# A chunked RWKV and two-MoE kernel on one core: bonus term of six units through TensorE, inverse decay on ScalarE, another start for units 0 and 1

## Chip, core and metric

One core of a Trainium2 chip (trn2) runs the whole program. The metric is the device time of one launch in microseconds. Engine names are those of the profile: PE is TensorE (PEld its weight loads), ACT is ScalarE, DVE is VectorE, POOL is GpSimd, SP is SyncE; the `q` of SPq or ACTq marks an engine's issue of DMAs.

## What is computed

A linear-attention recurrence with decay and a bonus term, then two MLPs on its output (batch 4, 8 heads, 768 steps, head size 48):

```python
for t in range(S):
    cur = einsum('bhd,bhe->bhde', u * kt, vt)            # bonus
    y[t] = einsum('bhd,bhde->bhe', rt, state + cur)
    state = wt[..., None] * state + einsum('bhd,bhe->bhde', kt, vt)
x = y.transpose(0, 2, 1, 3).reshape(3072, 384)
x = relu(x @ w_in) ** 2 @ w_out                          # d_ff 2048
out = ((x @ w_a) * (x @ w_b)) @ w_out2                   # d_ff 1536
```

All inputs are float32, uniform decays between 0.8 and 0.95.

## The kernel before

The sequence is cut into 6 chunks of 128 steps. A unit is one chunk of one batch, 24 in all, with 8 heads as 4 groups of 2. `prepare(i)` does the part of a unit that needs no TensorE. A forward scan on DVE (L197) gives the running product f of the decays; a reciprocal of its last column (L201) and a scan backwards (L202) give its inverse q. Then r is multiplied by f (L206), k by q (L208), and one Newton step corrects q (L209, L210); ACT squares f and q into a range check (L218). POOL multiplies r, k and u (L220, L221), DVE sums over the head (L223), and ACT writes that sum `dd` as a diagonal into the matrix A, one activation a head (L226): this is the bonus term. `scores(i)` makes the score matrices on PE (L239), transposes k (L243), and DVE copies the scores over A's diagonal under a mask (L247). `mix(i)` multiplies A with v (L267), adds the state's part from the second chunk on (L261), and makes the new state (L274, L292, L294). The result x is copied from PSUM (L284), and six small DMAs move the last 16 of each head pair into place (L287).

Units are gathered in tiles: tile 0 holds units 0 and 1 (256 tokens), five tiles hold four units, the last one two. The first MLP runs tile by tile in 16 steps: `hp` (L417 in tile 0, L311 to L313 after), its square on ACT and DVE (L423, L424; later L463, L464, L371, L372), and `acc` (L410; L311 to L313). While tile n runs, the units of tile n+1 are prepared. Tile 0 works in float32, the later ones split each operand into two fp32r parts and make three products. Weights arrive as 64-bit words and are decoded in four instructions, ACT, DVE, ACT, DVE (L41 to L44), two tiles of weights a step of tile 0. The second MLP starts when the first is through.

The program is written in this order, and a scheduler with its own cost estimates interleaves it on every engine; units 0 and 1 have higher priority (offset 100). On the chip each engine runs its instructions strictly in the order so found, so what waits holds everything behind it. Pools set the number of buffers: `A` 2, `fq` 1, PSUM 3 `acc`, 2 `mm` and 3 `at` banks.

Of the kernel before, what the change touches and what calls it, by code (L numbers as in the profile page):

```python
# [8 lines left out]
F32 = mybir.dt.float32  # L9
# [3 lines left out]
AF = mybir.ActivationFunctionType  # L13
ALU = mybir.AluOpType
AX = mybir.AxisListType

B, H, S, D = 4, 8, 768, 48
# [3 lines left out]
C = 128  # L21
# [3 lines left out]
G = 4  # L25
GP = 112
T = B * C
HP = 100
BURSTS = (0, 2, 4, 6, 7, 9, 11, 13)
LOW = 2.0 ** -52  # L30
LIM = 2.0 ** 102
# [40 lines left out]
def chunked_path(ctx, tc, flags, krT, wT, krn, vn, u, w1, w2, w3, w4, w5, out):  # L72
    nc = tc.nc
    pe, act, dve, pool, sync = nc.tensor, nc.scalar, nc.vector, nc.gpsimd, nc.sync
    PS = bass.MemoryType.PSUM

    const = ctx.enter_context(tc.tile_pool(name="const", bufs=1))
# [5 lines left out]
    at = ctx.enter_context(tc.tile_pool(name="at", bufs=1))  # L83
    dr = ctx.enter_context(tc.tile_pool(name="dr", bufs=1, space=bass.MemoryType.DRAM))
    p_acc = ctx.enter_context(tc.tile_pool(name="p_acc", bufs=3, space=PS))
    p_mm = ctx.enter_context(tc.tile_pool(name="p_mm", bufs=2, space=PS))
# [7 lines left out]
    mask = const.tile([128, 1, 128], F32, name="mask")  # L94
    d1 = const.tile([GP, G, C + 1], F32, name="d1")
    ones = const.tile([GP, 1], F32, name="ones")
    d2 = const.tile([GP, G, C + 1], F32, name="d2")
    half = const.tile([GP, 1, 2], F32, name="half")
    u_bc = const.tile([128, DM], F32, name="u_bc")
    chk = const.tile([GP, NU], F32, name="chk")  # L100
# [69 lines left out]

    loaded = {}

    def load_unit(i):
        b, c = units[i]
        w = ld.tile([GP, G * (C + 1) + 1], F32, tag="lw", name="lw")
        kr = ld.tile([GP, 2, G, C], F32, tag="lkr", name="lkr")
        v = ld.tile([128, H, D], F32, tag="vn", name="vn", bufs=3)
        nn = ld.tile([128, 2, H, D], F32, tag="nn", name="nn")
        r0 = b * S + c * C
        sync.dma_start(out=w, in_=wT[b, c])  # L180
        sync.dma_start(out=kr, in_=krT[b, c])
        sync.dma_start(out=v, in_=vn[r0:r0 + C].rearrange("p (h d) -> p h d", h=H))
        sync.dma_start(out=nn, in_=krn[r0:r0 + C].rearrange("p n (h d) -> p n h d", h=H))
        loaded[i] = w, kr, v, nn

    xt = {}
    tiles = [(0, 1)] + [tuple(range(i, i + 4)) for i in range(2, NU - 2, 4)] + [(NU - 2, NU - 1)]
    x0 = {}
    unit = {}

    def prepare(i):
        b, c = units[i]
        w, kr, v, nn = loaded.pop(i)
        k, r = kr[:, 0], kr[:, 1]
        fq = at.tile([GP, 2, G * (C + 1)], F32, tag="f", name="fq")
        f, q = (fq[:, n].rearrange("p (g t) -> p g t", g=G) for n in range(2))
        dve.tensor_tensor_scan(  # L197
            out=fq[:, 0], data0=w[:, :-1], data1=d1.rearrange("p g t -> p (g t)"),
            initial=0.0, op0=ALU.mult, op1=ALU.max,
        )  # L200
        dve.reciprocal(out=d2[:, :, C:], in_=f[:, :, C:])  # L201
        dve.tensor_tensor_scan(  # L202
            out=fq[:, 1, ::-1], data0=w[:, 1:][:, ::-1], data1=d2.rearrange("p g t -> p (g t)")[:, ::-1],
            initial=0.0, op0=ALU.mult, op1=ALU.add,
        )
        dve.tensor_tensor(out=r, in0=r, in1=f[:, :, 0:C], op=ALU.mult)  # L206
        e = w[:, 0:G * C].rearrange("p (g t) -> p g t", g=G)
        dve.tensor_tensor(out=k, in0=k, in1=q[:, :, 1:], op=ALU.mult)  # L208
        dve.tensor_tensor(out=e, in0=f[:, :, 1:], in1=q[:, :, 1:], op=ALU.mult)  # L209
        dve.scalar_tensor_tensor(  # L210
            out=k, in0=e, scalar=2.0, in1=k, op0=ALU.subtract, op1=ALU.mult, reverse0=True
        )
        pe2 = at.tile([GP, G, 2, 1], F32, tag="pe2", name="pe2", bufs=2)
        dve.tensor_tensor(
            out=pe2[:, :, :, 0], in0=f[:, :, C:C + 1].to_broadcast([GP, G, 2]),
            in1=half.to_broadcast([GP, G, 2]), op=ALU.mult,
        )
        act.activation(out=fq, in_=fq, func=AF.Square, accum_out=chk[:, i:i + 1])  # L218
        p = nn[:, 0]
        pool.tensor_tensor(out=p, in0=p, in1=u_h, op=ALU.mult)  # L220
        pool.tensor_tensor(out=p, in0=p, in1=nn[:, 1], op=ALU.mult)  # L221
        dd = at.tile([128, H, 1], F32, tag="dd", name="dd", bufs=2)
        dve.tensor_reduce(out=dd[:, :, 0], in_=p, axis=AX.X, op=ALU.add)  # L223
        A = at.tile([128, 2, G, C], F32, tag="A", name="A", bufs=2)
        for h in range(H):
            act.activation(out=A[:, h % 2, h // 2, :], in_=ident, func=AF.Copy, scale=dd[:, h])  # L226
        unit[i] = dict(k=k, r=r, v=v, A=A, pe2=pe2)
        if i + 2 < NU:
            load_unit(i + 2)

    def scores(i):

        b, c = units[i]
        st = unit[i]
        ps = [p_at.tile([128, G, C], F32, tag="at", name="ps") for _ in range(2)]
        for g in range(G):
            for j in range(2):
                s = slice(64 * j, 64 * j + D)
                pe.matmul(out=ps[j][:, g, :], lhsT=st["k"][s, g, :], rhs=st["r"][s, g, :], start=True, stop=True)  # L239
        if c < NC - 1:  # L240
            pt = p_at.tile([128, 4, C], F32, tag="at", name="pt")
            for g in range(G):
                pe.transpose(out=pt[:, g, 0:GP], in_=st["k"][:, g, :], identity=ident[:GP, :GP])  # L243

        def post():
            for j in range(2):
                dve.copy_predicated(st["A"][:, j], mask.bitcast(I32).to_broadcast([128, G, C]), ps[j])  # L247
            if c < NC - 1:
                st["kt"] = at.tile([128, G, GP], F32, tag="kt", name="kt")
                act.activation(out=st["kt"], in_=pt[:, :, 0:GP], func=AF.Copy)  # L250
        return post

    def mix(i):

        b, c = units[i]
        st = unit.pop(i)
        A, v, s = st["A"], st["v"], states[b]
        ps = p_at.tile([128, G, C], F32, tag="at", name="py")
        if c > 0:
            for g in range(G):  # L260
                pe.matmul(  # L261
                    out=ps[0:GP, g, :], lhsT=s[:, g].rearrange("p j d -> p (j d)")[:, 0:GP],
                    rhs=st["r"][:, g, :], start=(g == 0), stop=False, skip_group_check=True,
                )
        for g in range(G):
            for j in range(2):
                pe.matmul(  # L267
                    out=ps[64 * j:64 * j + D, g, :], lhsT=v[:, 2 * g + j, :], rhs=A[:, j, g, :],
                    start=(c == 0), stop=True, skip_group_check=True,
                )  # L270
        if c < NC - 1:
            pk = p_at.tile([128, G, 2, D], F32, tag="at", name="pk")
            for g in range(G):
                pe.matmul(out=pk[0:GP, g], lhsT=st["kt"][:, g, :], rhs=v[:, 2 * g:2 * g + 2, :], start=True, stop=True)  # L274

        def post():
            if i > 1:
                x = at.tile([128, G, C], F32, tag="x", name="xf", bufs=2)
            else:
                if i == 0:  # L280
                    x0[0] = xp.tile([128, G, 2, C], F32, tag="x", name="x0")
                x = x0[0][:, :, i, :]
            for rows in ((slice(0, GP),) if c > 0 else (slice(0, D), slice(64, GP))):
                act.activation(out=x[rows], in_=ps[rows], func=AF.Copy)  # L284
            for p0 in (0, 64):
                for m in range(3):
                    sync.dma_start(out=x[p0 + 48:p0 + 64, m], in_=x[p0 + 16 * m:p0 + 16 * m + 16, 3])  # L287
            if c < NC - 1:
                src = pk[0:GP]
                if c > 0:  # L290
                    t = at.tile([GP, G, 2, D], F32, tag="kt", name="t")
                    dve.tensor_tensor(out=t, in0=src, in1=s[:, :, :, 0:D], op=ALU.add)  # L292
                    src = t
                dve.tensor_tensor(  # L294
                    out=s[:, :, :, 0:D], in0=src, in1=st["pe2"].to_broadcast([GP, G, 2, D]), op=ALU.mult
                )
            return (lambda: split_x(i, x)) if i > 1 else None
        return post
# [14 lines left out]
        pe.matmul(out=out, lhsT=wt[:, 1, sl], rhs=rhs_hi, start=False, stop=last)  # L313


    load_unit(0)
    make_identity(nc, ident)
    for s in states:
        pool.memset(s, 0.0)
# [3 lines left out]
    )  # L323
    dve.memset(d1, LOW)
    dve.memset(d1[:, :, 0:1], 1.0)
    dve.memset(d2, 0.0)
    dve.memset(ones, 1.0)
    dve.memset(near, 0.4375)
    dve.memset(half, 0.0)
    dve.memset(half[0:64, :, 0:1], 1.0)  # L330
    dve.memset(half[64:GP, :, 1:2], 1.0)
    sync.dma_start(out=u_bc, in_=u.rearrange("h d -> (h d)").rearrange("(o n) -> o n", o=1).to_broadcast([128, DM]))
    load_unit(1)
    load_w1(2)
    tails = []
    with tc.high_priority(offset=HP):
        prepare(0)
    for i in range(2):
        with tc.high_priority(offset=HP):
            p = scores(i)  # L340
            if i == 0:
                prepare(1)
            p()
            mix(i)()
        decode_w1()
        decode_w1()

# [380 lines left out]
```

## Time and profile before

| | |
|---|---|
| median of three runs | 1030.08 us (1028.87 to 1030.48) |
| the profiled execution | 1029.76 us |
| its span, first to last instruction | 1028.1 us |
| PE busy | 984.1 us, 96% |
| DVE busy | 540.5 us, 53% |
| ACT busy | 448.3 us, 44% |
| POOL busy | 72.7 us, 7% |
| mean granted TensorE clock | 0.997 |

The shares are over the whole span, and the stages differ: in the first fifth DVE has most of its work, in the second half PE. Matmuls are pipelined and their ends are modelled, so a PE that shows as busy may be waiting between matmuls. A float32 matmul is recorded as two instructions.

### The profile page before, as it was taken

How to read it: one execution, taken by the hardware profiler on the slowest of the kernel's cores; microseconds unless marked ns; L12 is line 12 of the kernel's file. 1: busy time of each engine (PE TensorE's matmuls, PEld its weight loads, DVE VectorE, ACT ScalarE, POOL GpSimd, SP SyncE). 2: the span in 40 equal slices, each digit the busy share in tenths (PEclk: the TensorE clock that was granted, in tenths of full speed). 3: DMA queues.
4: the chain of work that ended last, by engine and by line, in shares of the span. 5: the costliest groups of instructions: out<-in, count | busy, mean ns of one | idle time of the engine just before them, and what ended most of it. 6: DMA issues, size and time to landing. Idle time of an engine off the chain costs nothing. (4 is left out here: it accounts for less than half of the span.)

```text
span 1028.1 us, 13834 instructions
## 1 busy us (share of the span) xinstructions
PE 984.1 (96%) x5250; PEld 834.4 (81%) x5250; DVE 540.5 (53%) x908; ACT 448.3 (44%) x930; POOL 72.7 (7%) x60
## 2 busy tenths in 40 slices
PE   3789999998999999999999999999999999999996
PEld 2577777777788888887889988888888888888885
DVE  8999999988856756644346622222222222222221
ACT  5788676777555444543336612222322312212211
POOL 4234201000100100000000000000000000000000
PEclk9999999999999999999999999999999999999998
DMA  9677237877422221201015400100100100000001
GB/s 274 218 254 244 67 95 254 258 257 244 146 83 64 77 67 54 65 21 54 23 46 155 132 1 2 61 1 21 41 1 1 41 1 16 27 1 32 0 1 34
DMA packets 47020, 88.15 MB, mean 86 GB/s; under 512 B 7008, under 2 KB 25568, under 8 KB 46944
## 3 DMA queue, kind: packets, MB, share of 16 engines
q1 hardware_dynamic: 40464, 77.74, 24.5%
q10 hardware_dynamic: 6480, 9.44, 2.6%
q8 instruction: 43, 0.70, 0.3%
q14 instruction: 33, 0.27, 0.1%
HBM read 69.46 MB, written 16.52 MB: 84 GB/s over the span
## 5 line engine op out<-in xcount | busy, mean ns | idle before, releaser
L536 DVE TENSOR_TENSOR t<-ap,t 128x512 f32<-128x512 f32 x72 | 49.8, 691 | 278.7 <-PE ap L313 278.7
L371 ACT ACTIVATE gh<-t 128x512 fp32r<-128x512 f32 (+1 forms) x168 | 102.4, 609 | 185.3 <-DVE t L536 127.0
L372 DVE TENSOR_TENSOR gl<-t,gh 128x512 fp32r<-128x512 f32 (+1 forms) x168 | 112.1, 667 | 74.7 <-ACT gh L371 74.4
L527 ACT ACTIVATE t<-bp 128x512 f32<-128x512 f32 x72 | 43.1, 598 | 160.4 <-PE bp L313 159.7
L311 PE MATMUL hp<-x,w 128*128 128x512 f32 (+1 forms) x288 | 109.3, 379 | 2.7 <-DVE t L464 2.7
L312 PE MATMUL acc<-gl,w 128*128 128x512 f32 (+1 forms) x288 | 108.2, 376 | 1.9 <-DVE gl L372 1.8
L313 PE MATMUL acc<-gh,w 128*128 128x512 f32 (+1 forms) x288 | 107.5, 374 | 0.0
L312 PE MATMUL hp<-x,w 128*128 128x512 f32 (+1 forms) x288 | 107.2, 372 | 0.0
L313 PE MATMUL hp<-x,w 128*128 128x512 f32 (+1 forms) x288 | 107.1, 372 | 0.0
L311 PE MATMUL acc<-gh,w 128*128 128x512 f32 (+1 forms) x288 | 102.6, 383 | 0.0
L464 DVE TENSOR_TENSOR t<-t,hp 128x512 f32<-128x512 f32 (+1 forms) x96 | 61.0, 635 | 74.0 <-ACT t L463 74.0
L518 PE MATMUL acc<-w,gh 128*128 128x384 f32 x288 | 96.8, 336 | 0.0
L519 PE MATMUL acc<-w,gh 128*128 128x384 f32 x288 | 96.7, 336 | 0.0
L520 PE MATMUL acc<-w,gl 128*128 128x384 f32 x288 | 95.1, 337 | 0.0
L463 ACT ACTIVATE t<-hp 128x512 f32<-128x512 f32 (+1 forms) x96 | 53.3, 555 | 83.2 <-PE hp L313 81.3
L313 PE MATMUL bp<-x,w 128*128 128x512 f32 x216 | 85.3, 395 | 0.0
L312 PE MATMUL bp<-x,w 128*128 128x512 f32 x216 | 85.1, 394 | 0.0
L312 PE MATMUL ap<-x,w 128*128 128x512 f32 x216 | 84.1, 390 | 0.0
L313 PE MATMUL ap<-x,w 128*128 128x512 f32 x216 | 84.1, 389 | 0.0
L311 PE MATMUL ap<-x,w 128*128 128x512 f32 x216 | 84.1, 389 | 0.0
L311 PE MATMUL bp<-x,w 128*128 128x512 f32 x216 | 83.8, 390 | 0.0
L311 PEld LDWEIGHTS hp<-x,w 128*128 128x128 f32 x288 | 54.2, 188 | 14.4 <-DVE t L464 4.3
(93 smaller groups left out, 1713.5 us busy)
## 6 DMA issues: line engine op xcount, KB each, us to landing
raw<-in_w SPq DMA_DIRECT2D x68, 384.0 KB, 4.7
lkr<-in_krT SPq DMA_DIRECT2D x24, 448.0 KB, 4.1
nn<-in_krn SPq DMA_DIRECT2D x24, 384.0 KB, 3.9
w2d<-f SPq DMA_DIRECT2D x36, 192.0 KB, 2.8
ws<-w2d SPq DMA_DIRECT2D x36, 192.0 KB, 2.5
lw<-in_wT SPq DMA_DIRECT2D x24, 226.2 KB, 3.4
vn<-in_vn SPq DMA_DIRECT2D x24, 192.0 KB, 2.8
out<-e ACTq DMA_DIRECT2D x24, 192.0 KB, 1.9
```

Of the source, the lines that this page charges most:

```text
L311: pe.matmul(out=out, lhsT=wt[:, 0, sl], rhs=rhs_hi, start=first, stop=False)
L312: pe.matmul(out=out, lhsT=wt[:, 0, sl], rhs=rhs_lo, start=False, stop=False)
L313: pe.matmul(out=out, lhsT=wt[:, 1, sl], rhs=rhs_hi, start=False, stop=last)
L371: act.activation(out=gh, in_=t, func=AF.Copy)
L372: dve.tensor_tensor(out=gl, in0=t, in1=gh.bitcast(F32), op=ALU.subtract)
L463: act.activation(out=t, in_=hp, func=AF.Relu)
L464: dve.tensor_tensor(out=t, in0=t, in1=hp, op=ALU.mult)
L518: pe.matmul(out=acc[t], lhsT=ph[:, sl], rhs=w_o[f][:, 0, :], start=(f == 0), stop=False)
L519: pe.matmul(out=acc[t], lhsT=ph[:, sl], rhs=w_o[f][:, 1, :], start=False, stop=False)
L520: pe.matmul(out=acc[t], lhsT=pl[:, sl], rhs=w_o[f][:, 0, :], start=False, stop=(f == 11))
L527: act.activation(out=bs, in_=bp, func=AF.Copy)
L536: dve.tensor_tensor(out=bs, in0=ap, in1=bs, op=ALU.mult)
```

## The change

For the first six units (`EARLY`), A is set to zero by POOL, POOL multiplies v by `dd` (`vd`, one buffer), and PE adds `vd` through the identity matrix in `mix`, eight matmuls a unit; the eight ACT writes of the diagonal are left out. The later units keep them. For all 24 units q is no longer made by reciprocal and scan: ACT takes Ln of f and Exp of its negative. Each unit loads its `nn` before its `vn`; for units 0 and 1 both go behind `u_bc`. Units 0 and 1 are written one after the other (prepare, scores, mix), and take PSUM banks of pools that are idle then.

```diff
+EARLY = 6
-    d2 = const.tile([GP, G, C + 1], F32, name="d2")
-    def load_unit(i):
+    def load_unit(i, late=None):
...
-        sync.dma_start(out=v, in_=vn[r0:r0 + C].rearrange("p (h d) -> p h d", h=H))
-        sync.dma_start(out=nn, in_=krn[r0:r0 + C].rearrange("p n (h d) -> p n h d", h=H))
+        def rest():
+            sync.dma_start(out=nn, in_=krn[r0:r0 + C].rearrange("p n (h d) -> p n h d", h=H))
+            sync.dma_start(out=v, in_=vn[r0:r0 + C].rearrange("p (h d) -> p h d", h=H))
+
         loaded[i] = w, kr, v, nn
+        if late is None:
+            rest()
+        else:
+            late.append(rest)
@@ prepare
-        dve.reciprocal(out=d2[:, :, C:], in_=f[:, :, C:])
-        dve.tensor_tensor_scan(
-            out=fq[:, 1, ::-1], data0=w[:, 1:][:, ::-1], data1=d2.rearrange("p g t -> p (g t)")[:, ::-1],
-            initial=0.0, op0=ALU.mult, op1=ALU.add,
-        )
+        act.activation(out=fq[:, 1], in_=fq[:, 0], func=AF.Ln)
+        act.activation(out=fq[:, 1], in_=fq[:, 1], func=AF.Exp, scale=-1.0)
...
-        for h in range(H):
-            act.activation(out=A[:, h % 2, h // 2, :], in_=ident, func=AF.Copy, scale=dd[:, h])
-        unit[i] = dict(k=k, r=r, v=v, A=A, pe2=pe2)
+        vd = None
+        if i < EARLY:
+            pool.memset(A, 0.0)
+            vd = at.tile([128, H, D], F32, tag="vd", name="vd")
+            pool.tensor_tensor(out=vd, in0=v, in1=dd.to_broadcast([128, H, D]), op=ALU.mult)
+        else:
+            for h in range(H):
+                act.activation(out=A[:, h % 2, h // 2, :], in_=ident, func=AF.Copy, scale=dd[:, h])
+        unit[i] = dict(k=k, r=r, v=v, A=A, pe2=pe2, vd=vd)
@@ scores and mix take their PSUM pool as an argument; in mix
-                    start=(c == 0), stop=True, skip_group_check=True,
+                    start=(c == 0), stop=st["vd"] is None, skip_group_check=True,
                 )
+            if st["vd"] is not None:
+                for j in range(2):
+                    pe.matmul(
+                        out=ps[64 * j:64 * j + D, g, :], lhsT=st["vd"][:, 2 * g + j, :], rhs=ident,
+                        start=False, stop=True, skip_group_check=True,
+                    )
@@ the start
-    load_unit(0)
+    late = []
+    load_unit(0, late)
...
-    dve.memset(d2, 0.0)
...
-    load_unit(1)
+    late[0]()
+    load_unit(1, late)
+    late[1]()
     load_w1(2)
     tails = []
-    with tc.high_priority(offset=HP):
-        prepare(0)
     for i in range(2):
         with tc.high_priority(offset=HP):
-            p = scores(i)
-            if i == 0:
-                prepare(1)
-            p()
-            mix(i)()
+            prepare(i)
+            scores(i, *((p_at, "at"), (p_acc, "acc"))[i])()
+            mix(i, *((p_mm, "mm"), (p_at, "at"))[i])()
         decode_w1()
         decode_w1()
```

Where these edits put the instructions is seen in the built programs. Lines of the changed kernel are some 10 to 17 higher. A scan stands in these lists as SCALAR_TENSOR_TENSOR `fq<-lw,d`.

DVE, the start of the program, units 0 and 1. Before:

```order
L197 SCALAR_TENSOR_TENSOR fq<-lw,d_133 112x516
L201 RECIPROCAL d_135<-fq 112x4
L206 TENSOR_TENSOR lkr<-lkr,fq 112x512
L223 TENSOR_REDUCE dd<-nn 128x8
L214 TENSOR_TENSOR pe_239<-fq,half 112x8
L202 SCALAR_TENSOR_TENSOR fq<-lw,d_135 112x516
L208 TENSOR_TENSOR lkr<-lkr,fq 112x512
L209 TENSOR_TENSOR lw<-fq 112x512
L210 SCALAR_TENSOR_TENSOR lkr<-lw,lkr 112x512
L247 COPY_PREDICATED A<-mask,ps 128x512 x2
```

And in the change:

```order
L203 SCALAR_TENSOR_TENSOR fq<-lw,d_133 112x516
L226 TENSOR_REDUCE dd<-nn 128x8
L209 TENSOR_TENSOR lkr<-lkr,fq 112x512
L217 TENSOR_TENSOR pe_282<-fq,half 112x8
L211 TENSOR_TENSOR lkr<-lkr,fq 112x512
L212 TENSOR_TENSOR lw<-fq 112x512
L257 COPY_PREDICATED A<-mask,ps 128x512 x2
L213 SCALAR_TENSOR_TENSOR lkr<-lw,lkr 112x512
```

Both pieces begin with unit 1's forward scan and hold unit 0's two copies under the mask (L247, now L257). Reciprocal and backward scan are gone, and unit 0's copies stand one instruction earlier than unit 1's last product.

ACT, from unit 0's diagonal to unit 1's k. Before:

```order
L226 ACTIVATE A<-ident,dd 128x128 x8
L41 ACTIVATE raw<-raw,near 128x384
L218 ACTIVATE fq,chk<-fq 112x1032
L250 ACTIVATE kt<-pt 128x448
L41 ACTIVATE raw<-raw,near 128x384 x2
```

And in the change, behind the same four instructions and a square (L221) of unit 0:

```order
L207 ACT_TABLE_LOAD
L207 ACTIVATE fq<-fq 112x516
L208 ACT_TABLE_LOAD
L208 ACTIVATE fq<-fq 112x516
L221 ACTIVATE fq,chk<-fq 112x1032
L42 ACTIVATE raw<-raw,near 128x384
L260 ACTIVATE kt<-pt 128x448
```

Each unit now has two table loads, one ahead of Ln (L207) and one ahead of Exp (L208); the whole program has 48 where it had one. The eight writes of the diagonal are gone for the early units.

PE, the end of unit 1 and the first `hp` of the MLP. Before:

```order
L243 MATMUL pt<-ident,lkr 128x112 x4
L267 MATMUL py<-A,vn 48x128
L417 MATMUL hp<-x_281,wf 128x256 x4
L267 MATMUL py<-A,vn 48x128 x6
L417 MATMUL hp<-x_281,wf 128x256 x2
```

And in the change:

```order
L432 MATMUL hp<-x_250,wf 128x256 x6
L278 MATMUL py<-A,vn 48x128 x2
L284 MATMUL py<-ident,vd 48x128 x2
L249 MATMUL ps<-lkr 128x128 x8
L432 MATMUL hp<-x_250,wf 128x256 x3
L425 MATMUL acc<-g,wf 128x256 x3
```

The first `hp` stands behind one of unit 2's eight products with v before; now it stands behind six of them and their six `vd` partners (L284), and the last two of each follow it.

## Rows read from the trace of the kernel before

**Rows 1.** The page, parts 1 and 2: engine totals, and busy tenths in 40 slices.
```profile
PE 984.1 (96%) x5250; PEld 834.4 (81%) x5250; DVE 540.5 (53%) x908; ACT 448.3 (44%) x930; POOL 72.7 (7%) x60
...
PE   3789999998999999999999999999999999999996
...
DVE  8999999988856756644346622222222222222221
```

**Rows 2.** Windows: stretch, length, then busy us (and instructions) of each engine.
```profile
core 0: us, PE busy (x) PEld busy (x) DVE busy (x) ACT busy (x) POOL busy (x), PEclk, DMA share, GB/s
0.00:43.50 43.50, 21.39 (x110) 17.02 (x110) 38.19 (x62) 25.75 (x61) 17.27 (x24) 1.00 0.76 236
43.50:117.50 74.00, 68.61 (x425) 56.73 (x425) 74.00 (x138) 58.60 (x140) 23.02 (x14) 1.00 0.70 222
117.50:200.00 82.50, 81.28 (x433) 63.61 (x431) 79.86 (x140) 61.85 (x133) 11.87 (x8) 1.00 0.55 179
200.00:300.00 100.00, 94.09 (x528) 74.97 (x529) 81.20 (x140) 63.33 (x134) 10.71 (x8) 1.00 0.60 190
```

**Rows 3.** Timeline of units 0 and 1: start, length, engine, line, instruction, idle before.
```profile
0.81 1.28 ACT L218 ACT_TABLE_LOAD   x1 [0.81 <-PEq L713]
...
2.67 0.53 POOL L319 MEMSET s<- 112x512 f32 x1
...
3.77 1.23 DVE L197 TENSOR_TENSOR_SCAN fq<-lw,d 112x516 f32<-112x516 f32 x1 [1.51 <-DMA lw<-in_wT]
...
5.26 1.23 DVE L202 TENSOR_TENSOR_SCAN fq<-lw,d 112x516 f32<-112x516 f32 x1
...
6.99 0.68 DVE L208 TENSOR_TENSOR lkr<-lkr,fq 112x512 f32<-112x512 f32 x1
...
9.05 2.08 PE L239 MATMUL ps<-lkr 48*128 48x128 f32 x16 [9.05 <-DVE lkr L210]
...
10.63 2.03 DVE L197 TENSOR_TENSOR_SCAN fq<-lw,d 112x516 f32<-112x516 f32 x1 [1.63 <-DMA lw<-in_wT]
...
14.15 1.77 POOL L220 TENSOR_TENSOR nn<-nn,u_bc 128x384 f32<-128x384 f32 x1 [2.58 <-DMA nn<-in_krn]
...
15.16 1.30 DVE L208 TENSOR_TENSOR lkr<-lkr,fq 112x512 f32<-112x512 f32 x1
...
18.52 1.33 DVE L247 COPY_PREDICATED A<-mask,ps 128x512 f32<-128x512 int32 x2
```

**Rows 4.** Groups of DVE by line, 0 to 118 us: count, busy us, mean ns.
```profile
L202 DVE TENSOR_TENSOR_SCAN fq<-lw,d 112x516 f32<-112x516 f32 x8 | 10.5, 1318 | 0.0
...
L201 DVE RECIPROCAL d<-fq 112x4 f32<-112x4 f32 x8 | 1.4, 170 | 0.1
```

**Rows 5.** Groups of ACT by line, 0 to 118 us.
```profile
L226 ACT ACTIVATE A<-ident,dd 128x128 f32<-128x128 f32 x72 | 22.2, 388 | 8.1 <-DVE dd L223 8.0
...
L218 ACT ACTIVATE fq<-fq 112x1032 f32<-112x1032 f32 x8 | 8.5, 1057 | 9.9 <-DVE lw L209 9.8
```

**Rows 6.** Timeline of PE: unit 2's and 3's products, the first `hp`, tile 1's first.
```profile
43.50 3.78 PE L417 MATMUL hp<-x,wf 128*128 128x256 f32 x8
...
59.74 1.08 PE L267 MATMUL py<-A,vn 128*48 128x128 f32 x16
...
117.52 0.59 PE L311 MATMUL hp<-x,w 128*128 128x512 f32 x1
```

**Rows 7.** Waits of PE, then of DVE, 230 to 340 us: total, times, longest.
```profile
PE ps L239 <- ACT xf L284: 2.6, 1, 2.6
PE hp L311 <- DVE t L464: 1.7, 2, 1.2
PE acc L312 <- DVE gl L372: 1.6, 1, 1.6
...
DVE t L464 <- ACT t L463: 10.3, 4, 4.2
...
DVE lkr L206 <- DMA lkr<-in_krT: 5.8, 4, 2.5
```

More of the change, by code (lines that the diff above doesn't have):

```diff
@@ L224, in prepare, with scores @@
         A = at.tile([128, 2, G, C], F32, tag="A", name="A", bufs=2)
-        for h in range(H):
-            act.activation(out=A[:, h % 2, h // 2, :], in_=ident, func=AF.Copy, scale=dd[:, h])
-        unit[i] = dict(k=k, r=r, v=v, A=A, pe2=pe2)
+        vd = None
[7 more added lines that the diff above has]
+        unit[i] = dict(k=k, r=r, v=v, A=A, pe2=pe2, vd=vd)
         if i + 2 < NU:
             load_unit(i + 2)
-    def scores(i):
+    def scores(i, pool=None, tag="at"):
         b, c = units[i]
         st = unit[i]
-        ps = [p_at.tile([128, G, C], F32, tag="at", name="ps") for _ in range(2)]
+        pool = pool or p_at
+        ps = [pool.tile([128, G, C], F32, tag=tag, name="ps") for _ in range(2)]
         for g in range(G):
@@ L240, in scores @@
         if c < NC - 1:
-            pt = p_at.tile([128, 4, C], F32, tag="at", name="pt")
+            pt = pool.tile([128, 4, C], F32, tag=tag, name="pt")
             for g in range(G):
@@ L251, in scores, with mix @@
         return post
-    def mix(i):
+    def mix(i, pool=None, tag="at"):
         b, c = units[i]
@@ L257, in mix @@
         A, v, s = st["A"], st["v"], states[b]
-        ps = p_at.tile([128, G, C], F32, tag="at", name="py")
+        pool = pool or p_at
+        ps = pool.tile([128, G, C], F32, tag=tag, name="py")
         if c > 0:
@@ L268, in mix @@
                     out=ps[64 * j:64 * j + D, g, :], lhsT=v[:, 2 * g + j, :], rhs=A[:, j, g, :],
-                    start=(c == 0), stop=True, skip_group_check=True,
+                    start=(c == 0), stop=st["vd"] is None, skip_group_check=True,
                 )
+            if st["vd"] is not None:
[4 more added lines that the diff above has]
+                    )
         if c < NC - 1:
-            pk = p_at.tile([128, G, 2, D], F32, tag="at", name="pk")
+            pk = pool.tile([128, G, 2, D], F32, tag=tag, name="pk")
             for g in range(G):
```

## Prediction

> **What bounds it now.** I read the page first: PE is busy for 96% of the span, DVE for 53%, ACT for 44% [rows 1]. Over the whole span this leaves little but PE's 44 us of idle time. The 40 slices say where that lies: PE begins at 3 and 7 tenths, while DVE stands at 8 or 9 tenths for the first eleven slices [rows 1]. So I went on by windows. From 43.5 us, where the first `hp` starts, to 117.5 us, where tile 1 starts [rows 6], DVE is busy for all 74.0 us, PE for 68.6, ACT for 58.6; to 200 us DVE has 79.9 of 82.5 [rows 2]. PE looks almost as full, but a matmul that waits inside its modelled length shows as busy. **Stage A (0 to 117.5 us) is bound by DVE**, and by the start-up chain before it is full: PE's first matmul comes at 9.05 us [rows 3]. Stage B (to 200 us) is bound by DVE and PE together. In stage C (to 300 us) DVE falls to 81% and PE still idles 5.9 us [rows 2]; the waits there are PE on DVE or ACT, and DVE 10.3 us on ACT's first copy of `hp` and 5.8 us on loads of k and r [rows 7]: latencies of a fixed order, not full engines. From 300 us on the slices show PE full, and nothing of the change makes PE's work there smaller.
>
> **The change, part by part.** The sum is made against the profiled execution, 1029.76 us; its span is 1028.1 us, and the median of the three runs, 1030.08 us, is 0.3 us above it. A measurement can tell about 0.2%, 2.1 us, from no change.
>
> *1. DVE loses the backward scan and the reciprocal.* In stage A there are eight of each, 10.5 us and 1.4 us [rows 4]. A reciprocal overlaps its neighbour by half, so I count 0.7. In a stage where DVE is full that is -11.2 us. The memset of `d2` also goes, but it stood ahead of DVE's 1.51 us wait for the first load [rows 3], so it is worth nothing.
>
> *2. The inverse on ACT.* Per unit ACT gets Ln, Exp and two table loads. The only table load in the trace takes 1.28 us [rows 3]; Ln and Exp over 516 columns I take at half the square over 1032 columns (1.06 us [rows 5]), 0.55 us each. A unit costs ACT 3.7 us. Up to the last step of tile 0 the lists hold 16 such activations and 15 loads more than before, 8.8 + 19.2 = 28.0 us; they hold 56 diagonal writes fewer (72 to 16) at 0.31 us (22.2 us for 72 [rows 5]), -17.3 us. Net +10.7 us, and six weight splits come ahead of that place, about 3 us. ACT's 84.4 us in stage A [rows 2] become about 98 of some 111 us: close to full, no longer cover for everything. The excess that the trace cannot show is whether a load costs ACT more than its 1.28 us, because what runs before it must end first. The bounds: nothing more, or once the length of the activation ahead of it, 0.55 us. I take 0.1.
>
> The Trainium skill ("ScalarE: Activation LUTs", What ACT_TABLE_LOAD costs) states 1283 ns for the load and about 1380 ns more for a drain, 2.66 us for a switch of sets. The load's figure agrees with the trace's row; of the drain no run here shows anything. By the page the 15 loads would take 39.9 us and not 19.2, and ACT would have 119 us of work instead of 98.
>
> *3. The start.* Unit 0's forward scan ends at 5.0 us, its backward one at 6.5 [rows 3]. By ACT: 5.0 + 0.55 + 1.28 + 0.55 = 7.4 us (the first load is early and hidden). The product with r fills part of it, and DVE's next product starts at 7.4 instead of 6.99: +0.4 us. For unit 1 the scan cannot start before its load lands at 10.63 us [rows 3]; it ends near 11.9, its Exp at 14.3, and DVE has only a reduction, one product and a tiny one in between: about 1.3 us idle. Together +2 us of DVE waiting (bounds: 0, if loads come earlier by the new order, and 4, if ACT is late by half a microsecond each time). In return unit 0's copies under the mask, at 18.52 us before [rows 3], move up in the list by one instruction, and unit 1 comes straight behind. Up to the copies of unit 2 that the first `hp` stands behind, DVE's list has lost four scans and reciprocals (-5.6 us) and, net, about two short instructions (-1); with +2 of waiting and three `vd` (+1.5, item 4) it gets there 3 us earlier, and PE then has twelve more small matmuls ahead of the first `hp` than before: 41 to 42 us instead of 43.5. This gain is part of item 1, not added to it.
>
> *4. POOL.* Six products `vd` of a size like L220's (1.77 us beside DVE work), and six memsets of twice the 0.53 us one [rows 3]. POOL has 40 us of work in stage A [rows 2], so its own time is cover; A's memset waits for PE to be through with the A of two units before, and the products with u stand behind it in POOL's queue, but they are made a unit ahead. What costs is DVE beside it: the same product took 0.68 us alone and 1.30 with POOL running, a scan 1.23 and 2.03 [rows 3]. So 0 to 0.8 us a `vd` on DVE; I take 0.5, +3 us (bounds 0 and 4.8). The memsets at the start stood beside DVE work of unchanged length; I take 0 for them, at most 0.8 each.
>
> The Trainium skill ("SBUF — State Buffer", Who interferes with whom) says that a DVE instruction with two SBUF inputs and a GpSimd one that reads SBUF exclude each other for a whole instruction, and that one that only writes does not. The first agrees with the 1.30 us; by it, if DVE always came second, six `vd` would cost 6 us or more, not 3.
>
> *5. PE.* Eight extra matmuls a unit: eight of the same shape took 1.08 us as 16 records [rows 6], so 6.5 us for six units. Three units fall ahead of the first `hp`, where PE mostly waits; the other three, 3.2 us, into a window in which PE idled 5.4 us [rows 2] and has some 2 us more room by the earlier `hp`. Cost 0; if the cover were gone, +3.2.
>
> *6. Loads.* `u_bc` and `nn` come ahead of `vn` for units 0 and 1: the same bytes, and POOL can start up to a microsecond earlier. Other banks for units 0 and 1: no instruction more. 0.
>
> Stage A: -11.2 + 2 + 3 = -6.2 us, and for ACT's fuller queue, in which decodes wait behind Ln and Exp, I add back 0.5 (bounds 0 and 6): **-5.7**.
>
> *7. Stage B.* Four units are prepared per tile: -4 x 1.4 = -5.6 us of DVE work at 97% load, but ACT gets +4 x 3.7 = 14.7 us on 61.9 of 82.5 [rows 2] and none of its diagonal writes back. Bounds -5.6 and +4; as ACT at 93% gives much of it away, **-1.5**.
>
> *8. Stage C and after.* DVE loses 1.4 us a unit, ACT holds its queue 3.7 us at a time. `hp` has two banks and `acc` follows two steps behind, so a few us of ACT are mostly hidden. Bounds: -5.9 (all PE idle there) and +5 (three of the waits in [rows 7] longer by half of 3.7). I take 0. From 300 us on PE is full: 0.
>
> Sum: -5.7 - 1.5 + 0 = -7.2, so 1029.8 - 7.2 = **1022.6 us**.
>
> **Rivals.**
>
> *ACT becomes the bound (slower).* In stage A ACT has 98 us of work and about 8 us at the start in which it waits for data (8.0 us ahead of the diagonal alone [rows 5]), 106 in all. If a load holds ACT for twice its row, 1.28 us more, 15 loads add 19 us: stage A ends at 125 us instead of 117.5, +7.5; stage B has 61.9 + 4 x 6.3 = 87 us of ACT against 82.5, +4.5. That is 1042 us. It decides from about 0.8 us a load (106 + 15 x 0.8 = 118); at 1.05 us it is 122 us in A and 86 in B, 1037 us. For it: the in-order queue, two loads a unit, Exp waiting for Ln on the same engine. Against it: the row of 1.28 us [rows 3]. The drain that the Trainium skill states (item 2) points to this rival and would make it 1043 us. Chance 0.25, with all results over +2.
>
> *The whole DVE saving arrives.* If `vd` collides little and ACT keeps up, A gives -10, B -5.6, C -1: 1013 us. For it: DVE at 100% in A, and PE with room. Against it: ACT at 88 to 93%. Chance 0.17.
>
> *Given back later.* Stage A ends earlier, but weights, k and r do not arrive earlier (DVE waits 5.8 us on them in C [rows 7]), and the waits in C grow by as much as A gained: 1028 to 1031 us, no change. Chance 0.13, of which a third is just outside 0.2% on the fast side.
>
> **How the numbers follow.** The forecast, -2.1 to -11 us, has 0.45. Faster: 0.45 + 0.17 + 0.04 = 0.66; same 0.09; slower 0.25. The range reaches from 1012 (nearly all savings) to 1037 (ACT bound with a load 1.05 us dearer), leaving out 0.05 below and 0.14 above. The likeliest case alone is 1018 to 1027.
>
> **What would show it.** Right: tile 1's first matmul at 110 to 113 us; the first `hp` at 41 to 42; DVE still full from 20 us on; ACT near 88% in A; table loads with 1.28 us and no gap behind them; no wait of PE on `vd`. Wrong: gaps of a microsecond around each load, DVE's first wait in A naming L207 or L208, or DVE products beside `vd` twice as long each time.

## The result, and the profile after

The changed kernel takes 1043.31 us (median of four runs, 1039.55 to 1045.86), the kernel before beside it 1029.88 us; the ratio is 1.0131, with a 95% interval of 1.0106 to 1.0157. It is slower by 13 us, where 7 us less were forecast, and lies above the whole range. The profiled execution took 1043.58 us, with a span of 1041.9 us.

The page of the changed kernel, parts 1 and 2 (engine totals, then busy tenths in 40 slices; PEclk is the granted clock):

```profile
PE 993.5 (95%) x5346; PEld 841.7 (81%) x5346; DVE 511.9 (49%) x859; ACT 519.8 (50%) x977; POOL 80.2 (8%) x72
...
PE   3789999888999999999999999999999999999996
...
DVE  6898997887755565653336732222322222221221
ACT  5889989887756675663235721321312312312211
...
PEclk9789999999899999999999999999999999999999
```

Against [rows 1] DVE lost 29 us of work, and ACT has 519.8 us where it had 448.3 us. DVE's digits are no longer 8 and 9 throughout the first eleven slices: the work that it lost did not shorten this stretch, DVE waits there instead.

Where the time went is read from the places where the tiles start, in the timeline of PE (us; the first `hp` of tile 0, then the first `hp` of tiles 1, 2 and 3). "One set" is an experiment told below, the changed kernel with a single table load; "other order" is another, the kernel before with its instructions in another order.

| profiled execution | first `hp` | tile 1 | tile 2 | tile 3 |
|---|---|---|---|---|
| before | 43.5 | 117.5 | 199.5 | 291.4 |
| changed | 44.1 | 119.8 | 211.5 | 306.6 |
| one set | 39.5 | 111.1 | 198.5 | 290.9 |
| other order | 42.8 | 116.1 | 203.9 | 299.7 |

Tiles 3, 4 and 5 take 84.7, 82.9 and 72.7 us in all four, and in every other profile of this study. All of the loss lies ahead of tile 3: 2.3 us in stage A (to tile 1), 9.7 us in tile 1, 3.2 us in tile 2. After tile 5 1.4 us come back, so that the span is 13.8 us longer. Each row of the table is one execution, and executions of one kernel differ (the changed one's by 6.3 us), so a difference of a us or two between rows need not be the kernel's. The windows of the changed kernel at these places (stretch, length, busy us and instructions of each engine, granted clock, DMA share, GB/s):

```profile
0.00:44.06 44.06, 21.69 (x172) 17.99 (x173) 32.16 (x54) 29.77 (x43) 21.95 (x29) 0.89 0.82 229
44.06:119.80 75.74, 68.69 (x412) 55.62 (x411) 69.88 (x128) 68.22 (x137) 23.22 (x18) 0.93 0.65 206
119.80:211.50 91.70, 84.77 (x472) 66.57 (x470) 77.94 (x141) 80.99 (x163) 9.66 (x8) 1.00 0.63 199
211.50:306.60 95.10, 91.03 (x490) 73.20 (x491) 68.43 (x116) 73.23 (x139) 11.77 (x9) 0.95 0.54 172
```

The kernel before has for tile 1:

```profile
117.50:199.50 82.00, 80.78 (x431) 63.35 (x429) 79.36 (x139) 61.73 (x132) 11.87 (x8) 1.00 0.55 178
```

In stage A ACT has 29.77 + 68.22 = 98.0 us of work, to the microsecond what was forecast; but the stage lasts 119.8 us, so ACT is busy for 82% of it and DVE, with 102.0 us, for 85%. No engine is full. Up to tile 2 DVE does 32.16 + 69.88 + 77.94 = 180.0 us of work, where before it did 38.19 + 74.00 [rows 2] + 79.36 = 191.5 us. It was relieved by 11.5 us, and its idle time rose from 8.0 to 31.5 us.

The timeline of the changed kernel for units 0 and 1 shows how (start, length, engine, line, instruction, idle before and what ended it):

```profile
5.06 0.63 ACT L207 ACTIVATE fq<-fq 112x516 f32<-112x516 f32 x1 [2.96 <-DVE fq L203]
5.71 1.28 ACT L208 ACT_TABLE_LOAD   x1
7.00 0.63 ACT L208 ACTIVATE fq<-fq 112x516 f32<-112x516 f32 x1
7.67 0.69 DVE L211 TENSOR_TENSOR lkr<-lkr,fq 112x512 f32<-112x512 f32 x1 [1.74 <-ACT fq L208]
...
9.74 2.08 PE L249 MATMUL ps<-lkr 48*128 48x128 f32 x16 [9.74 <-DVE lkr L213]
...
12.90 1.23 DVE L203 TENSOR_TENSOR_SCAN fq<-lw,d 112x516 f32<-112x516 f32 x1 [3.21 <-DMA lw<-in_wT]
14.17 0.63 ACT L207 ACTIVATE fq<-fq 112x516 f32<-112x516 f32 x1 [2.65 <-DVE fq L203]
14.66 1.21 POOL L232 TENSOR_TENSOR vd<-vn,dd 128x384 f32<-128x384 f32 x1 [2.03 <-DVE dd L226]
14.82 1.28 ACT L208 ACT_TABLE_LOAD   x1
...
16.11 0.63 ACT L208 ACTIVATE fq<-fq 112x516 f32<-112x516 f32 x1
16.78 0.69 DVE L211 TENSOR_TENSOR lkr<-lkr,fq 112x512 f32<-112x512 f32 x1 [0.89 <-ACT fq L208]
```

Ln, load, Exp: the load stands between the two and cannot be hidden, since both are on ACT and Exp needs what Ln wrote. DVE's product waits for Exp. The load is 1.28 us long and Exp begins 0.01 us behind it. Unit 1's w lands at 12.90 us, 2.3 us later than before [rows 3]. The new load order is at most a part of why: in both kernels this load is the sixth that SP issues, at 3.16 us, and the scan behind it starts at 10.9 to 12.9 us in the eight profiles of this study with the new order, at 10.4 to 11.7 us in the nine with the old one.

The groups of ACT up to 120 us (count, busy us, mean ns of one, idle before):

```profile
L207 ACT ACT_TABLE_LOAD x8 | 10.3, 1283 | 1.3 <-PEq L728 0.8 <-DVE fq L203 0.4
L208 ACT ACT_TABLE_LOAD x8 | 10.3, 1283 | 0.1
...
L207 ACT ACTIVATE fq<-fq 112x516 f32<-112x516 f32 x8 | 5.1, 634 | 5.7 <-DVE fq L203 5.6
L208 ACT ACTIVATE fq<-fq 112x516 f32<-112x516 f32 x8 | 5.1, 633 | 0.1
```

And the waits of DVE up to tile 2 (total, times, longest):

```profile
DVE fq L203 <- DMA lw<-in_wT: 5.3, 2, 3.2
DVE lkr L211 <- ACT fq L208: 4.6, 5, 1.7
DVE f L43 <- ACT raw L42: 4.3, 4, 2.0
DVE lw L212 <- ACT fq L208: 4.1, 4, 1.4
DVE fq L203 <- ACT fq L221: 2.9, 3, 1.6
```

The two on L208 are new. DVE's waits for ACT's part of a decode and for its square, 4.3 and 2.9 us here, were short in the trace of before up to tile 2:

```profile
DVE f L42 <- ACT raw L41: 0.6, 1, 0.6
DVE fq L197 <- ACT fq L218: 0.4, 1, 0.4
```

DVE and ACT now hand a unit to and fro, each with a queue in a fixed order, and each loses time to the other without being full.

### The profile page after: what moved, and what is told of

Same layout as the page of the kernel before. It is cut to its first block, busy times and chain, and to the rows that moved or that the text cites. A ratio compares the mean times of both kernels' runs of the same rounds, so it can differ in the third digit from the quotient of the medians.

```text
span 1041.9 us, 14024 instructions
## 1 busy us (share of the span) xinstructions
PE 993.5 (95%) x5346; PEld 841.7 (81%) x5346; DVE 511.9 (49%) x859; ACT 519.8 (50%) x977; POOL 80.2 (8%) x72
## 5 line engine op out<-in xcount | busy, mean ns | idle before, releaser
L330 PE MATMUL acc<-gh,w 128*128 128x512 f32 (+1 forms) x288 | 108.2, 376 | 0.0
L328 PE MATMUL acc<-gh,w 128*128 128x512 f32 (+1 forms) x288 | 106.2, 389 | 0.7 <-ACT ev L413 0.7
```

Of the source, the lines that this page charges most:

```text
L328: pe.matmul(out=out, lhsT=wt[:, 0, sl], rhs=rhs_hi, start=first, stop=False)
```

## The experiments

The theories were named ahead of the runs. **L**: the table loads lengthen ACT's queue, and what hangs on it. **P**: the added matmuls and the new start. **W**: handing the inverse to ACT at all, loads or not. Times are medians; a ratio is always to the kernel before, run beside it on the same chip, with its 95% interval. Not all runs were on one chip, so ratios of different paragraphs compare less closely than their intervals say.

**Inverse back on DVE.** The changed kernel with reciprocal and scan of before. Here, and in "`vd` alone" below, `vd` is written over the used half of `nn`, for want of room.

```diff
-        act.activation(out=fq[:, 1], in_=fq[:, 0], func=AF.Ln)
-        act.activation(out=fq[:, 1], in_=fq[:, 1], func=AF.Exp, scale=-1.0)
+        dve.reciprocal(out=d2[:, :, C:], in_=f[:, :, C:])
+        dve.tensor_tensor_scan(
+            out=fq[:, 1, ::-1], data0=w[:, 1:][:, ::-1], data1=d2.rearrange("p g t -> p (g t)")[:, ::-1],
+            initial=0.0, op0=ALU.mult, op1=ALU.add,
+        )
-            vd = at.tile([128, H, D], F32, tag="vd", name="vd")
+            vd = nn[:, 1]
```

> The change with the inverse made on VectorE again (reciprocal and backward scan), so one table load instead of 48; vd is written over the used-up half of nn, since d2 needs its room back. Theory L (the table loads fill ScalarE's queue, and VectorE and TensorE wait for it): the loss goes, 1022 to 1030 us, granted clock back near 0.997. Theory P (the added matmuls, the new start and the idle gaps they leave for TensorE's clock are the loss): it stays, 1038 to 1045 us. Theory W (handing the inverse to ScalarE at all, two more waits a unit, is the loss, loads or not): as L here.

Measured: 1041.88 us, 1.0112 (1.0092 to 1.0132). The rest of the change, start and `vd`, costs 11.5 us beside an inverse on DVE. By itself this speaks for P; the next run shows that it is not the whole.

**One table set.** The changed kernel, with one line ahead of everything that loads a set which holds both functions.

```diff
+    act.preload_act_table_set("natural_log_exp_and_others")
```

> The change with one table set that has both Ln and Exp loaded ahead of everything: 1 load instead of 48, 47 x 1.28 = 60 us less of ScalarE, all else as in the change. Theory L: 1015 to 1026 us, below before. Theory P: 1038 to 1045 us. Theory W: 1034 to 1042 us, as the waits stay.

Measured: 1028.98 us, 0.9996 (0.9979 to 1.0012). The instructions stand in the same order on every engine as in the changed kernel, but for 47 loads that are gone; so the difference, 1.35% or 13.9 us (1.0131 against 0.9996, from two sets of runs), is the price of 47 loads, and no other order plays into it. The windows of this kernel at its own tile starts:

```profile
0.00:39.45 39.45, 20.02 (x172) 16.50 (x172) 32.13 (x56) 21.31 (x37) 22.86 (x29) 0.91 0.89 246
39.45:111.10 71.65, 66.32 (x411) 54.31 (x410) 70.09 (x127) 57.69 (x128) 25.15 (x19) 0.95 0.70 223
111.10:198.50 87.40, 83.57 (x471) 66.79 (x471) 78.14 (x141) 71.09 (x156) 10.16 (x8) 1.00 0.66 209
198.50:290.90 92.40, 89.78 (x491) 71.93 (x491) 69.72 (x118) 61.94 (x131) 14.36 (x10) 0.96 0.56 177
```

DVE's work up to tile 2 is 32.13 + 70.09 + 78.14 = 180.4 us, within 0.4 us of the changed kernel's; tile 2 starts 13.0 us earlier. So nearly all of the price is idle time of DVE, 31.5 us against 18.1 us. By stage the two profiles differ by 8.7 us in A (19.2 us of loads more), 4.3 us in tile 1 and 2.7 us in tile 2. Of the 8.7 us, 1.65 us is unit 1's w, which lands earlier in this profile (no price of the table loads: this scan starts at 10.74 us in a profile with 48 of them, the inverse alone below, and at 12.63 us in one with a single load, the inverse back on DVE):

```profile
11.25 1.42 DVE L203 TENSOR_TENSOR_SCAN fq<-lw,d 112x516 f32<-112x516 f32 x1 [2.88 <-DMA lw<-in_wT]
```

About 7 us in A are left for the loads. Its waits of DVE up to tile 2:

```profile
DVE fq L203 <- DMA lw<-in_wT: 4.9, 2, 2.9
DVE f L43 <- ACT raw L42: 3.5, 4, 1.9
DVE lkr L209 <- DMA lkr<-in_krT: 3.0, 5, 1.0
...
DVE lkr L211 <- ACT fq L208: 0.4, 1, 0.4
```

The waits on Exp (L208), 4.6 and 4.1 us with the loads, are 0.4 us in all without them. The wait for a decode stays (3.5 us), so that one is not the loads'. Theory L holds for this part, but it had promised 1015 to 1026 us, a gain over the kernel before, and there is none.

**The inverse alone**, on the kernel before, with the compiler's 48 loads, and the same **under one set**.

```diff
-        dve.reciprocal(out=d2[:, :, C:], in_=f[:, :, C:])
-        dve.tensor_tensor_scan(
...
-        )
+        act.activation(out=fq[:, 1], in_=fq[:, 0], func=AF.Ln)
+        act.activation(out=fq[:, 1], in_=fq[:, 1], func=AF.Exp, scale=-1.0)
...
+    act.preload_act_table_set("natural_log_exp_and_others")
```

(the last line in the second alone)

> The kernel before with the inverse on ScalarE (48 loads) and nothing else of the change. Theory L: slower, and more than the change, since the early units' diagonals stay on ScalarE too: 1042 to 1055 us. Theory P: 1028 to 1033 us. Theory W: 1038 to 1050 us.

> The kernel before with the inverse on ScalarE under one table set (1 load). Theory L: 1020 to 1029 us, 24 x 1.4 us of VectorE saved where it is the bound. Theory P: 1022 to 1031 us. Theory W: 1034 to 1045 us.

Measured: 1038.22 us, 1.0060 (1.0038 to 1.0083), and 1027.43 us, 0.9957 (0.9937 to 0.9977). Again the order of the instructions is the same in both, and 47 loads cost 1.03%, 10.6 us. Theory W falls: with one load the inverse on ACT is a gain. This version beats both kernels. Theory L has its range in the second only: with 48 loads it had expected more than the changed kernel's time, and the inverse alone takes less.

**Start alone, `vd` alone**, each with the inverse on DVE. The first is the changed kernel with `EARLY = 0` and the inverse of before; the second is the kernel before with `vd` for six units (over `nn`). Theory **S**: the start is the 11.5 us; theory **V**: `vd` is.

```diff
-EARLY = 6
+EARLY = 0
```

(the first, against the kernel with the inverse back on DVE)

> The kernel before with only the change's start (load order, other PSUM banks, units 0 and 1 one after the other); inverse on VectorE, diagonals on ScalarE. The runs so far: start and vd together, without ScalarE's inverse, cost 12 us. Theory V (the six vd cost it: GpSimd beside VectorE, and matmuls): 1027 to 1033 us here. Theory S (the start costs it: the order it gives the weights and units): 1036 to 1043 us.

> The kernel before with only the six units' bonus term through TensorE (vd over the used-up half of nn). Theory V: 1036 to 1043 us. Theory S: 1028 to 1034 us.

Measured: 1037.23 us, 1.0074 (1.0049 to 1.0099), and 1040.62 us, 1.0098 (1.0063 to 1.0134). Both cost by themselves, so neither theory holds, and the costs do not add: 0.74 + 0.98 = 1.72%, where both together have 1.12%.

**The same two under one set.**

> The change's start and the inverse on ScalarE under one table set, without vd. With the inverse alone under one set 1027.4 us, with start and vd too 1029.0. Theory V: 1020 to 1027 us. Theory S: 1029 to 1036 us.

> vd (its own tile) and the inverse on ScalarE under one table set, without the change's start. Theory V: 1029 to 1036 us. Theory S: 1020 to 1027 us.

Measured: 1029.82 us, 0.9985 (0.9959 to 1.0011), and 1028.35 us, 0.9989 (0.9971 to 1.0007). With the inverse on ACT the same edits cost about 0.3% above the inverse alone (0.9957, from another set of runs), not 0.7 to 1.0%. Neither V nor S has both of its ranges here.

**Parts of the start, and a neutral one.** Two kernels split the start: the load order alone, and the written order with its banks alone. The third changes nothing that is computed or loaded, only the priority offset of units 0 and 1, and with it the order on PE, DVE, ACT and SP. The fourth puts the load order into the fastest version. The first two have no `vd`. Theories **D** (late loads), **B** (order and banks), **R** (any other order of the scheduler costs some tenths of a per cent).

```diff
-HP = 100
+HP = 20
```

(the third)

> The kernel before with the other load order alone (nn ahead of vn in every unit, for units 0 and 1 both behind u_bc); inverse, bonus term, banks and written order as before. What it must explain: the whole start cost 0.74% alone. Theory D (the loads: unit 1's w lands later, so DVE's full list starts later): this one costs it, ratio 1.005 to 1.010, tile 1 starts 4 us or more late. Theory B (one-by-one handing over and banks): ratio 0.998 to 1.003. Theory R (any order of the scheduler other than that of before costs some tenths of a per cent, wherever it comes from): 1.003 to 1.010 here and in the two other kernels with the inverse on DVE.

> The kernel before with units 0 and 1 written one after the other on idle banks; loads, inverse and bonus term as before. Theory D: 0.998 to 1.003. Theory B: 1.005 to 1.010. Theory R: 1.003 to 1.010.

> The kernel before with the priority offset of units 0 and 1 at 20 instead of 100: the same instructions, in another order. Theories D and B say nothing of it and would leave it at 0.998 to 1.003, unless unit 0 or 1 is late. Theory R: 1.003 to 1.010, with tiles 3 to 6 of unchanged length and the loss ahead of tile 3's start.

> The fastest so far (inverse on ACT under one table set, nothing else) with the other load order. Theory D: slower than 0.9957 by 0.5% or more, so 1.001 or above. Theory B: 0.995 to 0.998. Theory R: anything between 0.993 and 1.001, and no sign that can be told ahead.

Measured: load order 1033.40 us, 1.0030 (1.0008 to 1.0052); written order and banks 1031.72 us, 1.0002 (0.9983 to 1.0020); neutral 1036.63 us, 1.0051 (1.0034 to 1.0069); load order in the fastest version 1030.08 us, 0.9990 (0.9967 to 1.0013). The neutral one tells most: the same instructions in another order cost 0.5%, lost in tiles 1 and 2. Its windows (first `hp` to tile 1, tile 1, tile 2):

```profile
42.81:116.14 73.33, 69.72 (x410) 56.95 (x411) 73.33 (x133) 57.46 (x135) 20.94 (x14) 0.98 0.71 220
116.14:203.91 87.77, 86.18 (x438) 67.85 (x437) 78.70 (x143) 61.88 (x139) 7.89 (x6) 0.96 0.54 171
203.91:299.74 95.83, 90.18 (x493) 70.79 (x493) 81.40 (x138) 61.52 (x132) 16.51 (x9) 0.96 0.63 202
```

Tile 1 takes 87.8 us instead of 82.0 with about the same work of DVE, 78.70 us against 79.36. Where it is lost is less sure than that it is: this profile was granted 0.96 of the clock in both tiles, the one of before 1.00, and 0.04 of 87.8 us is up to 3.5 us. The 0.5% itself stands on nine runs with a mean clock of 0.990, against 0.992 of before beside them. R has the sign in this one and in the load order, and it alone allows 0.9990 for the fourth; the written order alone costs nothing, so "any other order" is too strong. D and B together give 0.3% where the whole start gave 0.74%: that remainder has no part of its own.

**Weights earlier.** Up to tile 2 the one-set kernel shows ACT waiting 19.7 us for weight loads, the kernel before 7.3 us. Theory **M**: this takes back what DVE saved. Three kernels ask for weights one tile further ahead: the one-set kernel, the inverse alone under one set, and the kernel before as control.

```diff
-        load_w1(3)
+        load_w1(4)
...
-    load_w1(2)
+    load_w1(3)
```

> The change under one table set, with first-MLP weights asked for four tiles ahead instead of three. Theory M (DVE's saved work turns into waits for weights that do not land earlier): the waits of ACT on raw up to tile 2 fall from 19.7 us to 10 or less and the time falls by 3 us or more, ratio 0.997 or below. Theory R (the gain goes to the order of the scheduler, with no one resource behind it): the waits may fall, the time stays within 0.998 to 1.003.

> The inverse alone on ACT under one table set (ratio 0.9957), with weights four tiles ahead. Theory M: below 0.9935. Theory R: 0.994 to 0.999.

> The control: the kernel before with weights four tiles ahead. It waits for them only 7.3 us up to tile 2, with DVE full. Theory M: 0.999 to 1.002, since DVE is the bound. Theory R: 1.000 to 1.010.

Measured: 1032.55 us, 1.0029 (1.0006 to 1.0053); 1034.25 us, 1.0048 (1.0026 to 1.0070); 1040.18 us, 1.0096 (1.0065 to 1.0127). Waits of ACT, 0 to 200 us, in the inverse alone under one set, without earlier weights:

```profile
ACT raw L41 <- DMA raw<-in_w: 21.0, 20, 2.4
```

With them:

```profile
ACT raw L41 <- DMA raw<-in_w: 10.9, 17, 1.3
```

The wait fell by half, and the kernel became 0.9% slower (0.9957 to 1.0048). The control, which waits less for weights, lost 1.0% by the same edit; so the edit has a price of its own, and beside it the shorter wait shows no gain. Theory M has none of its three ranges, and nothing here shows that wait of ACT to be more than slack. In the one-set kernel the wait did not fall at all (20.1 us), so that run alone would have told nothing. R has its range in that run and in the control; the inverse alone with earlier weights is slower than R allowed.

## Why the prediction was wrong

From the kernel before to the changed one the ratios make a chain in three links: start and `vd` +1.12% (11.5 us), the inverse from DVE to ACT with one load -1.16% (12 us), 47 further loads +1.35% (13.9 us). The forecast had a place for each; the second came out near its size, the other two did not. The sizes depend on the order in which the links are taken: with the inverse first it is -0.43%, and start and `vd` then +0.39%.

- **Item 1, DVE's relief: right in sign, its size in part by luck.** -11.2 in A and about -1.5 behind it were written down; the link measures 12 us here, and 4 us where nothing else of the change stands beside it. Six pairs of this study differ by the inverse, those with `vd` also by where `vd` lies (0 and -0.43%, start 0.74 and -0.15, `vd` 0.98 and -0.11, both 1.12 and -0.04, load order 0.30 and -0.10, earlier weights 0.96 and 0.48): ACT under one set is better by 0.4 to 1.2% in each, 0.74% in the mean.
- **Item 2: the work was right, its price was not.** ACT's 98 us in A came true. The loads took 1.283 us in the mean of 48. 46 of them begin within 0.02 us of the end of what runs ahead of them on ACT, and behind 46 the next activation begins 0.01 us later; behind the other two it waits for DVE's scan, 2.96 and 2.65 us. Ln and Exp took 0.63 us, where half of the square gave 0.55.
- **"For ACT's fuller queue I add back 0.5 (bounds 0 and 6)" is the step that failed.** The profiles with and without the loads differ by 8.7 us in stage A (about 7 without the later w), and by 4.3 and 2.7 us in tiles 1 and 2, where items 7 and 8 had the loads inside -1.5 and 0. With the +2 of item 3, the waits of units 0 and 1, A had 2.5 us for all of it; 4.6 us (3.0 without the w) were gone by the first `hp`. I asked whether ACT would be full, and as it was not (82%), I let its load count as cover. But a load between Ln and Exp stands in a chain from DVE's scan to DVE's product, and DVE's list had next to nothing to put there: I had written of 1.3 us idle for unit 1 and left the other units out. Of 19.2 us of added loads in A, some 7 us reached the end of the stage.
- **Items 3 to 6, start and `vd`: too cheap.** `vd` was put at 3 us and the start at nothing (the +2 of item 3 is waiting for ACT's inverse); beside an inverse on DVE they cost 11.5 us. Beside one on ACT they cost 4 us (0.9957 to 0.9996), close to the 3. The single prices hold: in the changed kernel DVE's instructions beside the six `vd` are 2.2 us longer in all than the shortest of their kind in the same trace, `vd` is 1.2 us long in the median, and no wait of PE names it. What was most likely missed is the order: each edit makes the scheduler write another one, and another order alone costs 0.5% in the neutral run (1.0% in the control, which also asks for weights earlier). That the order is what start and `vd` cost is argued, not shown.
- **Item 3, the times of the start.** The first `hp` was expected at 41 to 42 us; it came at 44.1, with one set at 39.5. "Bounds 0, if loads come earlier by the new order" did not come true: unit 1's w was issued no earlier, and landed 2.3 us later in this profile.
- **Items 7 and 8.** With one set stage A ends 6.4 us earlier (-5.7 forecast), and tile 1 then takes 5.4 us longer (-1.5 forecast). Part of this is work that moved: the records of `pk`, the new state, are 24 in tile 1 before and 32 with one set (windows of these alone: busy us and instructions of PE, of its weight loads and of DVE), one unit more. Before:

```profile
117.50:199.50 82.00, 3.13 (x24) 2.81 (x24) 1.63 (x3) 1.00 0.55 178
```

With one set:

```profile
111.10:198.50 87.40, 4.25 (x32) 3.59 (x32) 2.20 (x4) 1.00 0.66 209
```

Three slips in the working changed no step. [rows 7] is from 230 to 340 us; in stage C itself DVE waits 5.9 us for the copy of `hp` and 3.5 us for k and r, not 10.3 and 5.8. By the terms of the first rival a load 1.38 us dearer gives 1044 us, not 1043. And 1018 to 1027 us is -2.8 to -11.8 us, not -2.1 to -11.

The rival "ACT becomes the bound" had the time (1037 to 1042 us) and the wrong mechanism: it needed a load of twice its row, and ACT full. Its condition was "from about 0.8 us a load"; the loads were no dearer by anything, and the loss came all the same. "Given back later" is what the one-set kernel does; that late weights are the reason, the last three runs do not bear out. The list of what would show it was half right: of the "wrong" signs, DVE's first wait behind that for the first w names L208, as was written; but there were no gaps around the loads, 1.28 us and nothing behind them, which stood under "right".

The Trainium skill ("ScalarE: Activation LUTs", What ACT_TABLE_LOAD costs) has about 1380 ns of drain with each load; the trace does not agree, as ahead of 46 and behind 46 of the loads there is no room for one. The same page (Table sets: the hidden batching unit) says that Ln and then Exp need one load, as one set holds both. As built, the changed kernel had two a unit; with that set loaded ahead the profile has one load in all, and the runs put 13.9 and 10.6 us on the rest.

What stays open: which order costs what. That other orders of the same instructions cost 0.5% is shown; why the start or `vd` costs 0.7 to 1.0% beside DVE's inverse and 0.3% beside ACT's is not shown. The profile of the inverse back on DVE has one lead: its tile 1 takes 95.0 us, and there PE waits longest for ACT's copy of x, where the profile of before has no wait of PE above 0.9 us in tile 1:

```profile
PE pt L257 <- ACT xf L305: 5.9, 1, 5.9
```

In the runs with `vd` and DVE's inverse `vd` also lies over `nn`, and no run tests that by itself. That a full DVE forgives no order is only argued.

## What to carry to other kernels

When work moves from a full engine to one with room, price the way there and back, not only the room: two handings over and all that stands between them on the other engine's queue, for each unit, against what the first engine can do meanwhile. Before an activation goes to ACT, look in the built program for table loads, and put functions that follow each other under one set. Where a scheduler orders the program, run the same instructions in another order once: that spread, here 0.5% (1.0% with weights also asked for earlier), is what a gain of 0.7% on paper has to be held against.

## What the runs showed that was not expected

TensorE's granted clock. In the profiled execution of before it is 1.00 in all windows ahead of 300 us [rows 2]; in the changed kernel it is 0.89, 0.93 and 0.95 in three of four. That profile of before is on the high side: its mean is 0.997, and 88 other runs of the same kernel have 0.985 to 0.998, 0.992 in the mean. Windows of 5 us of the changed kernel show a fall behind idle time of PE:

```profile
20.00:25.00 5.00, 5.00 (x48) 4.40 (x46) 4.95 (x10) 4.60 (x10) 1.53 (x2) 1.00 1.04 235
25.00:30.00 5.00, 1.97 (x20) 1.42 (x16) 4.57 (x6) 4.90 (x8) 4.88 (x5) 1.00 0.82 237
30.00:35.00 5.00, 4.84 (x44) 4.38 (x46) 5.00 (x11) 2.08 (x5) 1.32 (x2) 0.66 0.60 175
35.00:40.00 5.00, 2.37 (x22) 1.62 (x21) 3.44 (x7) 4.91 (x9) 2.32 (x3) 0.81 0.63 205
40.00:45.00 5.00, 5.00 (x32) 4.33 (x32) 4.19 (x8) 4.09 (x6) 1.57 (x2) 0.51 0.79 245
```

PE is busy for 1.97 of 5 us and is then granted less, down to about the lower level, 1.2 GHz, from 40 to 45 us, while it is busy. The kernel before has a like gap at the same place and keeps 2.4 GHz in its profiled execution:

```profile
25.00:30.00 5.00, 2.84 (x13) 2.37 (x12) 5.00 (x6) 1.44 (x5) 2.22 (x2) 1.00 0.24 73
```

The other order has a fall of its own in tile 1, behind a stretch in which PE is busy for 3.72 of 5 us:

```profile
121.00:126.00 5.00, 3.72 (x22) 2.86 (x20) 5.00 (x10) 3.07 (x8) 1.38 (x2) 1.00 0.41 131
126.00:131.00 5.00, 4.84 (x18) 3.67 (x16) 5.00 (x10) 4.81 (x11) 0.84 (x1) 0.50 0.13 36
```

The clock is not the main part of what made the changed kernel slow: one set has 0.91, 0.95 and 0.96 in the same stages and is as fast as before, and the start under one set, with a mean of 0.981 in its profile, is too (0.9985). It may be a small part. Over the 88 runs of the kernel before a mean clock lower by 0.01 goes with 3.4 us more, with a correlation of -0.5. The changed kernel's four runs have 0.983 in the mean, those of one set 0.987, those of the inverse back on DVE 0.982. At that rate, an estimate, 3 of its 13 us would go with the clock, 1.3 us of the 13.9 of the loads, and about 3 us of the 11.5 of start and `vd`. Whether the clock costs this or only falls where PE waits anyway was not measured by itself.
